# Sparse attention and a mixture of experts: stage two asks for each split weight one product ahead, and the planner's costs of a weight's scale change

## The chip, the cores and the metric

The kernel runs on one core of one Trainium2 chip. The metric is the device time of one execution in microseconds (us). TensorE (PE) multiplies matrices and loads their weights, VectorE (DVE), ScalarE (ACT) and GpSimd (POOL) work on tiles, and SyncE (SP) issues the DMAs.

## What is computed

First attention over blocks, for 4 batches of 8 heads, 768 positions and 64 values a head; then its result x, 3072 rows of 512, goes through a gate that is balanced over rows and columns, and through all 8 experts. Cut to what matters:

```python
scores = np.where(mask, scale * np.matmul(q, k.T), -1e9)     # mask from sampled_blocks
attn = softmax(scores) @ v                                   # -> x, 3072 x 512
logits = x @ w_gate
P = np.exp(logits - logits.max())
for _ in range(8):
    P /= P.sum(1, keepdims=True) + 1e-09
    P /= P.sum(0, keepdims=True) + 1e-09
    P *= N / E
for e in range(E):
    h = np.maximum(x @ w1[e], 0.0)                           # w1[e]: 512 x 1024
    out += P[:, e:e + 1] * (h @ w2[e])                       # w2[e]: 1024 x 512
```

## The kernel before

**Numbers.** Every float32 operand is split into two float16 parts, a high and a low one, and a product is three matmuls (high x high, high x low, low x high). A 2 x 2 block product is made from seven products of sums of blocks instead of eight; they are numbered 0 to 6 and run in the order 0, 1, 5, 6, 3, 4, 2. So each expert has seven split weights `w1p` and seven `w2p`, and each batch of x has seven split inputs `xp`.

**The attention** is written out by hand as a table of turns: `at(T, rank, function)`. At turn -20 the scale of the first q and k (`scale_qk`, L619 to L626) is made on DVE, and at turn -21 `lay_fence` (L488 to L515) builds the mask's fence from the sampled blocks, also on DVE. The q and k of the first head are then cast (ACT, L640), split (DVE, L644) and turned by DMA (L650).

**The experts.** A step i is expert e = i // 4 and batch b = i % 4. `stage1(i, qi)` makes a quarter of h: seven products into PSUM tiles `p` (L1192; four banks), which DVE and ACT combine (L1204, L1239), and ten or so operations on POOL and DVE that form and split seven `h` tiles. `stage2(i, p)` multiplies the `h` of product p with `w2p[p]` for three pairs of row tiles (L1309, PSUM tiles `py`, four banks) and DVE adds each into `acc` (L1332; in the first expert ACT writes the first product's, L1329). The main loop (L1372) runs the seven stage2 products of step i, with the four quarters of stage1 of step i + 1 between them, so PE has both kinds of work at hand.

**The change of expert.** In the last batch of an expert the next w2 is loaded (L177) and measured: eight partial maxima on ACT (L108, `mx_w`), the maximum of the eight on DVE (`whole`, L194, `ma_w`), its spread over all partitions by a transposition on PE into a `p` bank (`spread`, L114, `all_w`), and seven small DVE operations that make the scale (`power`, L200 to L206, `sw`). POOL forms the five sums of blocks that the seven products need (L1071, into `r` and `t`), and for each product ACT writes the high half of `w2p[p]` (L1056) and DVE the low half (L1060). w1 goes the same way (`arena` and `attic` are its split tiles).

**The planner.** These steps stand in a queue (`Slots`). `tick` is called once after each product, with the time that PE and DVE are taken to need; a step of the lazy queue is run at a tick when its turn has come, when `gap` ticks have passed since the last lazy step, and when the engine that it costs is not more than 1.0 us ahead of PE by the planner's account (`fits`). A step planned with no cost always fits. `need(key)` runs all that stands in the queue up to that key at once. `stage2(i, p)` needs the split of product p right before its matmuls. `not_earlier` keeps a step of a weight behind what its engine has in the program ahead of it, and a scheduler then orders each engine's instructions.

## Time and profile before

| | us |
|---|---|
| median of 3 runs | 2264.57 |
| lowest and highest | 2260.46, 2267.06 |
| the profiled execution | 2263.39 |
| its span | 2261.6 |
| PE busy | 2168.9 (96%) |
| DVE busy | 1883.2 (83%) |
| ACT, POOL busy | 1317.3 (58%), 1309.7 (58%) |
| stage two's matmuls, L1309, x8064 | 946.3 |
| stage one's matmuls, L1192, in four groups of one shape, the three largest | 411.5, 409.7, 146.3 |

A busy time is the union of an engine's instructions, so PE lacks 93 us of the span. A share of the whole span says little here: attention, the first expert and the later experts have different limits, and a wait counts only where PE has nothing else to run.

### The profile page before, as it was taken

What the parts mean: (1) busy time and instruction counts of PE and PEld (TensorE: products, weight loads), DVE (VectorE), ACT (ScalarE), POOL (GpSimd) and SP (SyncE); (2) the same over time, 40 slices, a digit from 0 to 9 for tenths busy, and PEclk for the clock granted to TensorE, in tenths of its full rate; (3) what the DMA queues carried; (4) which work ended last, traced back from release to release, by engine and by line L of the source; (5) the groups of instructions that cost most, each with busy time, mean ns of one, the idle gap of its engine ahead of it and who ended that gap; (6) DMA issues with size and microseconds to landing.
All of it is one profiled execution on the core that took longest, in us unless ns stands there. A gap on an engine that the chain in (4) does not pass through costs nothing.

```text
span 2261.6 us, 47616 instructions
## 1 busy us (share of the span) xinstructions
PE 2168.9 (96%) x18892; PEld 1599.6 (71%) x18892; DVE 1883.2 (83%) x3339; ACT 1317.3 (58%) x2435; POOL 1309.7 (58%) x1331
## 2 busy tenths in 40 slices
PE   6999999889998999999999999999999999999999
PEld 3777666657775777677777777777777777777777
DVE  8889999787888878887888788878887888788876
ACT  5998888755457644654465446544654465446442
POOL 2123445585548564866486648655866586658553
PEclk9999999999999999999999999999999999999999
DMA  7667866313112211221212121212121212121221
GB/s 165 138 141 152 199 131 141 122 57 115 50 50 87 87 50 66 71 87 50 84 53 87 50 87 50 87 50 87 50 87 50 87 50 87 50 87 57 78 78 50
DMA packets 195349, 192.39 MB, mean 85 GB/s; under 512 B 132124, under 2 KB 150580, under 8 KB 195124
## 3 DMA queue, kind: packets, MB, share of 16 engines
q1 hardware_dynamic: 194560, 189.30, 28.9%
q8 instruction: 148, 2.42, 0.4%
q14 instruction: 77, 0.63, 0.1%
q10 hardware_dynamic: 564, 0.03, 0.0%
HBM read 140.54 MB, written 17.30 MB: 70 GB/s over the span
## 4 chain that ended last, share of the span: by engine, by line
PE 72%; DVE 11%; POOL 9%; ACT 4%; issue 3%; DMA 1%; SPq 0%; POOLq 0%; DVEq 0%
PE py L1309 31%; PE p L1192 31%; POOL r L1071 3%; PE u L753 3%; DVE top L671 2%; POOL h L1224 2%; PE t L695 2%; PE t L698 2%; PE m L662 2%; PE m L665 2%; DVE acc L1332 1%; DVE attic L1060 1%; POOL s L1266 1%; DVE h L1224 1%; POOL a L1078 1%
## 5 line engine op out<-in xcount | busy, mean ns | idle before, releaser
L1309 PE MATMUL py<-w2p,h 128*128 128x256 f16 x8064 | 946.3, 273 | 30.3 <-DVE acc L1332 14.1
L1309 PEld LDWEIGHTS <-h 128*128 128x128 f16 x8064 | 788.2, 98 | 166.5 <-issue 32.1
L1332 DVE SCALAR_TENSOR_TENSOR acc<-py,spare,acc 128x256 f32<-128x256 f32 (+1 forms) x840 | 455.6, 580 | 61.4 <-PE py L1309 57.8
L1224 POOL TENSOR_TENSOR h<-u,h 128x384 f16<-128x384 f32 x128 | 118.7, 928 | 583.5 <-ACT h L1214 566.7
L1192 PEld LDWEIGHTS <-attic 128*128 128x128 f16 x3072 | 300.4, 98 | 191.7 <-issue 12.8
L1192 PE MATMUL p<-arena 128*128 128x384 f16 x2304 | 411.5, 327 | 9.0 <-DVE arena L1060 4.4
L1192 PE MATMUL p<-attic 128*128 128x384 f16 x2304 | 409.7, 326 | 5.4 <-ACT a L1239 2.0
L1192 PEld LDWEIGHTS <-arena 128*128 128x128 f16 x2304 | 225.6, 98 | 144.0 <-issue 9.6
L1214 ACT ACTIVATE h<-c 128x384 f16<-128x384 f32 x256 | 133.2, 520 | 313.8 <-DVE c L1204 240.4
L1204 DVE SCALAR_TENSOR_TENSOR a<-p,a 128x384 f32<-128x384 f32 x384 | 210.8, 549 | 20.3 <-PE p L1192 15.3
L671 DVE TENSOR_REDUCE top<-m 128x1 f32<-128x768 f32 x192 | 181.7, 951 | 27.8 <-PE m L665 26.8
L703 ACT ACTIVATE pe<-t,qk 128x768 int32<-128x768 f32 x192 | 172.3, 898 | 47.0 <-PE t L698 44.5
L1214 ACT ACTIVATE h<-r 128x384 f16<-128x384 f32 x256 | 132.2, 519 | 64.2 <-POOL r L1078 59.7
L1078 POOL TENSOR_TENSOR c<-c,r 128x384 f32<-128x384 f32 x128 | 158.9, 1242 | 10.0
L1078 POOL TENSOR_TENSOR r<-s,r 128x384 f32<-128x384 f32 x128 | 153.2, 1197 | 10.0
L1192 PE MATMUL p<-arena,attic 128*128 128x384 f16 x768 | 146.3, 326 | 3.8 <-DVE a L1204 3.8
L1204 DVE SCALAR_TENSOR_TENSOR r<-p,a 128x384 f32<-128x384 f32 x128 | 70.7, 552 | 93.5 <-PE p L1192 73.7
L1214 ACT ACTIVATE h<-s 128x384 f16<-128x384 f32 x128 | 66.8, 522 | 134.4 <-POOL s L1266 134.4
L1266 POOL TENSOR_TENSOR s<-a,u 128x384 f32<-128x384 f32 x128 | 134.5, 1051 | 17.5 <-ACT a L1263 17.4
L1078 POOL TENSOR_TENSOR a<-a,r 128x384 f32<-128x384 f32 x128 | 135.8, 1061 | 9.4
L662 PE MATMUL m<-kt,qt 128*128 128x512 f16 (+1 forms) x384 | 128.4, 334 | 11.0 <-DMA kt<-ks 7.9
L1071 POOL TENSOR_TENSOR r<-r 128x256 f32<-128x256 f32 (+1 forms) x106 | 119.5, 1145 | 33.0 <-DVE arena L1060 33.0
(206 smaller groups left out, 3736.9 us busy)
## 6 DMA issues: line engine op xcount, KB each, us to landing
arena<-xd SPq DMA_DIRECT2D x128, 384.0 KB, 4.0
attic<-xd SPq DMA_DIRECT2D x96, 384.0 KB, 4.1
r<-in_moe_w_dram SPq DMA_DIRECT2D x16, 2048.0 KB, 9.1
arena<-in_q_dram SPq DMA_DIRECT2D x16, 384.0 KB, 4.4
arena<-in_k_dram SPq DMA_DIRECT2D x16, 384.0 KB, 4.6
arena<-in_v_dram SPq DMA_DIRECT2D x4, 1536.0 KB, 8.3
xd<-xs_t SPq DMA_DIRECT2D x16, 384.0 KB, 3.5
out_dram<-acc SPq DMA_DIRECT2D x48, 128.0 KB, 1.7
```

Of the source, the lines that this page charges most:

```text
L662: nc.tensor.matmul(sc[:, lo:hi], lhsT=qt[:, 0, c], rhs=ka[:, lo:hi], start=True, stop=False)
L671: nc.vector.tensor_reduce(out=tops[n][:, c : c + 1], in_=sc[:, :S], axis=AX.X, op=ALU.max)
L703: nc.scalar.activation(pe, sc[:, :S], AF.Exp, bias=EXP_SHIFT, scale=qk[n // 2][3])
L1071: lambda c=c: Pinned.gpsimd.tensor_tensor(out=out[:, c], in0=x[:, c], in1=y[:, c], op=op),
L1078: nc.gpsimd.tensor_tensor(out=out, in0=x, in1=y, op=ALU.subtract)
L1192: nc.tensor.matmul(ps, lhsT=w1p[p][:, l, kc, fs], rhs=xp[p][:, r, kc], start=(kc == 0 and m == 0), stop=(kc == KH - 1 and m == 2),)
L1204: nc.vector.scalar_tensor_tensor(out=t, in0=ps, scalar=HDOWN, in1=other, op0=ALU.mult, op1=ALU.add)
L1214: nc.scalar.activation(h[:, 0], src, AF.Relu if relu else AF.Copy)
L1224: eng.tensor_tensor(out=h[:, 1], in0=src, in1=h[:, 0], op=ALU.subtract)
L1266: nc.gpsimd.tensor_tensor(out=s1, in0=a1, in1=u3, op=ALU.add)
L1309: nc.tensor.matmul(py, lhsT=hs[i, p, kc][:, l, tsl], rhs=w2p[p][:, r, kc], start=(kc == 0 and m == 0), stop=(kc == KF // 2 - 1 and m == 2),)
L1332: nc.vector.scalar_tensor_tensor(out=dst, in0=src, scalar=c, in1=dst, op0=ALU.mult, op1=ALU.add)
```

## The change

Four lines. `lay_fence` moves from turn -21 to -20. The maximum of the eight partial maxima is queued without a cost (0.1 us of DVE before), and the spread of every weight follows after a gap of 5 ticks, that of the second expert's w2 too (14 before). And in an expert's first batch (`b == 0`) `stage2` needs the split of its own product and that of the one after it in the order 0, 1, 5, 6, 3, 4, 2.

```diff
-        at(-21, LATER, lay_fence)
+        at(-20, LATER, lay_fence)
@@ scale_w
-        slots.add(whole, key, 1, True, dve=0.1)
-        slots.add(spread, key, 1, True, gap=14 if which == 2 and e == 1 else 5)
+        slots.add(whole, key, 1, True)
+        slots.add(spread, key, 1, True, gap=5)
@@ stage2
+    SECOND = (0, 1, 5, 6, 3, 4, 2)
+
     def stage2(i, p):
         e, b = divmod(i, B)
         if p not in (0, 1, 3):
             slots.need(("sum", i))
         slots.need(("h", i, p))
-        slots.need(("w2", e, p))
+        ahead = SECOND.index(p)
+        for k in SECOND[ahead : ahead + 2 if b == 0 else ahead + 1]:
+            slots.need(("w2", e, k))
```

Since four lines are added, a line of the kernel before from L1294 on stands four lines later in the changed one (L1309 is L1313, L1332 is L1336).

**DVE at the change to the fifth expert** (e = 4, i = 16). w2p_8081 is the split weight of product 0 and w2p_8082 that of product 1; r_17_0, a_17_0 and u_17_0 are combinations of the quarter of stage one that runs beside it, h_... low halves of h, and acc_8118<-py_0_... the accumulations of product 0. Before:

```order
L1060 SCALAR_TENSOR_TENSOR w2p_8081<-r_4_18880,sw_4_18885,w2p_8081 128x1024
L1224 TENSOR_TENSOR h_8105<-s_16_3_19436,h_8105 128x384
L1204 SCALAR_TENSOR_TENSOR u_17_0_19597<-p_17_0_19598,a_17_0_19568 128x384
...
L1332 SCALAR_TENSOR_TENSOR acc_8118<-py_0_0_19471,spare_19467,acc_8118 128x512 x2
L1332 SCALAR_TENSOR_TENSOR acc_8118<-py_0_1_19487,spare_19467,acc_8118 128x512 x2
L1332 SCALAR_TENSOR_TENSOR acc_8118<-py_0_2_19503,spare_19467,acc_8118 128x512 x2
L1060 SCALAR_TENSOR_TENSOR w2p_8082<-r_4_18880,sw_4_18885,w2p_8082 128x1024
```

Now, on the same engine at the same place:

```order
L1060 SCALAR_TENSOR_TENSOR w2p_8081<-r_4_18880,sw_4_18885,w2p_8081 128x1024
L1060 SCALAR_TENSOR_TENSOR w2p_8082<-r_4_18880,sw_4_18885,w2p_8082 128x1024
L1204 SCALAR_TENSOR_TENSOR r_17_0_19586<-p_17_0_19587,a_17_0_19577 128x384
L1204 SCALAR_TENSOR_TENSOR a_17_0_19577<-p_17_0_19597,a_17_0_19577 128x384
L1336 SCALAR_TENSOR_TENSOR acc_8118<-py_0_0_19477,spare_19467,acc_8118 128x512 x2
```

The split of product 1 has moved from behind all six accumulations of product 0 to a place ahead of them and ahead of the combinations r_17_0 and a_17_0.

**PE at the change to the second expert** (e = 1, i = 4). all_w_1 is the spread of the maximum of w2, p_4_2, p_4_3 and p_5_0 are products of three successive quarters of stage one. Before:

```order
L1192 MATMUL p_4_3_11328<-attic 128x384
L1192 LDWEIGHTS attic
L1192 MATMUL p_4_3_11328<-attic 128x384
L114 MATMUL all_w_1_11353<-ident,ma_w_1_10790 128x128
L1192 LDWEIGHTS arena
```

Now:

```order
L1192 MATMUL p_4_2_11158<-attic 128x384
L1192 LDWEIGHTS attic
L1192 MATMUL p_4_2_11158<-attic 128x384
L114 MATMUL all_w_1_11224<-ident,ma_w_1_10790 128x128
L1192 LDWEIGHTS arena
```

The spread has moved from the end of quarter p_4_3 to its beginning, 42 matmuls earlier. At the experts after the third the same instruction of w2 moves 106 matmuls earlier, to a place in front of the third quarter; there the 36 matmuls of product 4 and two of product 2 of stage two, which came beside and behind that quarter, now stand ahead of it.

**DVE at the start.** L619 is the first operation of the scale of the first q and k, L490 the first of the fence. Now:

```order
L481 TENSOR_SCALAR qs_109<-attic 128x24 x6
L619 TENSOR_REDUCE qk_0_178<-u_143 128x2
L620 TENSOR_SCALAR qk_0_178<-qk_0_178 128x2
L622 TENSOR_SCALAR qk_0_178<-qk_0_178 128x2
L623 RECIPROCAL qk_0_179<-qk_0_178 128x2
L624 TENSOR_SCALAR qk_0_179<-qk_0_179 128x2
L625 TENSOR_SCALAR qk_0_178<-qk_0_178 128x2
L626 TENSOR_SCALAR qk_0_180<-qk_0_178 128x1
L490 CAST attic<-attic 24x72
```

Before, L490 followed L481, and the scale came after all of the fence.

## Rows read from the trace of the kernel before

**Rows 1.** Stretches in us: length, busy per engine (instructions), clock, DMA share, GB/s.
```profile
440.00:530.00 90.00, 78.96 (x557) 54.97 (x554) 72.25 (x116) 52.89 (x104) 68.62 (x66) 0.98 0.24 86
...
690.00:720.00 30.00, 21.76 (x130) 13.35 (x129) 24.21 (x42) 24.38 (x55) 28.82 (x30) 0.89 0.30 93
...
880.00:980.00 100.00, 92.99 (x702) 68.39 (x701) 87.85 (x150) 60.31 (x120) 70.27 (x67) 1.00 0.15 53
...
1335.00:1435.00 100.00, 95.30 (x720) 69.89 (x718) 90.21 (x154) 57.12 (x114) 72.17 (x69) 1.00 0.15 50
```

The engines stand in the order PE, PE's weight loads, DVE, ACT, POOL.

**Rows 2.** Timeline of PE, fifth expert: start, us, instruction, count, [idle before, releaser].
```profile
1364.33 3.09 PE L1192 MATMUL p<-arena 128*128 128x384 f16 x18
...
1403.25 3.76 PE L1309 MATMUL py<-w2p,h 128*128 128x256 f16 x33 [1.18 <-DVE w2p L1060]
...
1417.19 1.47 PE L1309 MATMUL py<-w2p,h 128*128 128x256 f16 x12 [1.69 <-DVE acc L1332]
...
1424.51 0.92 PE L1309 MATMUL py<-w2p,h 128*128 128x256 f16 x7 [0.97 <-ACT w2p L1056]
...
2079.29 3.76 PE L1309 MATMUL py<-w2p,h 128*128 128x256 f16 x33 [1.19 <-DVE w2p L1060]
```

**Rows 3.** Timeline of DVE, fifth expert.
```profile
1397.43 4.03 DVE L1332 SCALAR_TENSOR_TENSOR acc<-py,spare,acc 128x512 f32<-128x512 f32 x6
1401.38 1.82 DVE L1060 SCALAR_TENSOR_TENSOR w2p<-r,sw,w2p 128x1024 f16<-128x1024 f32 x1
```

**Rows 4.** Timeline of ACT, fifth expert.
```profile
1367.21 0.63 ACT L108 ACTIVATE unread<-r 128x512 bf16<-128x512 f32 x1
1367.75 0.19 ACT L108 ACTIVATION_READ_ACCUMULATOR unread<-r 128x1 f32 x1
...
1388.13 1.15 ACT L1056 ACTIVATE w2p<-r,sw 128x1024 f16<-128x1024 f32 x1
```

**Rows 5.** Line L1060: count, duration in ns min/median/max, first and last start.
```profile
L1060 DVE SCALAR_TENSOR_TENSOR w2p<-r,sw,w2p x48: 1266/1451/2093, 468.2 to 2111.7; 128x1024 f16<-128x1024 f32 x48
```

**Rows 6.** The stretch around the fifth expert's splits, columns as in rows 1.
```profile
1388.20:1424.50 36.30, 32.48 (x246) 23.86 (x244) 33.75 (x52) 19.09 (x34) 35.67 (x35) 1.00 0.04 16
```

**Rows 7.** Tile mx_w (the partial maxima): its reader, columns as in rows 5.
```profile
L194 DVE TENSOR_REDUCE ma_w<-mx_w x16: 142/152/163, 301.3 to 2056.2; 128x1 f32<-128x8 f32 x16
```

**Rows 8.** Waits of PE from 880 to 980: us in total, times, longest.
```profile
PE py L1309 <- DVE acc L1332: 3.0, 2, 1.7
PE py L1309 <- DVE w2p L1060: 1.7, 1, 1.7
```

**Rows 9.** Timeline of PE, second expert.
```profile
690.60 3.09 PE L1192 MATMUL p<-attic 128*128 128x384 f16 x18
...
709.08 0.47 PE L114 MATMUL all_w<-ident,ma_w 128*128 128x128 f32 x1 [7.16 <-DVE ma_w L194]
```

**Rows 10.** Timeline of ACT, second expert.
```profile
696.25 0.52 ACT L1214 ACTIVATE h<-c 128x384 f16<-128x384 f32 x1
696.68 0.61 ACT L108 ACTIVATE unread<-r 128x512 bf16<-128x512 f32 x1
```

**Rows 11.** Timeline of POOL, second expert.
```profile
702.54 1.00 POOL L1078 TENSOR_TENSOR c<-c,r 128x384 f32<-128x384 f32 x1
```

**Rows 12.** One microsecond after that wait, columns as in rows 1.
```profile
709.00:710.00 1.00, 0.92 (x4) 0.53 (x5) 0.75 (x2) 1.00 (x3) 0.92 (x2) 0.50 0.00 0
```

**Rows 13.** Timeline of PE, first expert.
```profile
486.06 1.47 PE L1309 MATMUL py<-w2p,h 128*128 128x256 f16 x12 [0.54 <-ACT w2p L1056]
...
498.32 1.15 PE L1192 MATMUL p<-arena,attic 128*128 128x384 f16 x5 [2.67 <-DVE a L1204]
```

**Rows 14.** Timeline of DVE, first expert.
```profile
491.82 0.56 DVE L1204 SCALAR_TENSOR_TENSOR c<-p,u 128x384 f32<-128x384 f32 x1 [2.66 <-POOL s L1266]
...
494.60 2.02 DVE L1060 SCALAR_TENSOR_TENSOR w2p<-t,sw,w2p 128x1024 f16<-128x1024 f32 x1
```

**Rows 15.** Timeline of DVE, start.
```profile
11.90 0.62 DVE L644 SCALAR_TENSOR_TENSOR qs<-arena,qk,qs 128x384 f16<-128x384 f32 x1 [0.68 <-ACT qs L640]
```

## The prediction

> **What bounds the kernel now.** I read the stretches of the span first, to see where TensorE (PE) is not busy, and then the timeline of PE with the releaser of each wait. From 40 us on PE is nearly always busy, and what it lacks lies where one expert's weights give way to the next: 11.0 of 90 us at the first expert, 8.2 of 30 us at the second, 7.0 of 100 us at the third and 4.7 of 100 us at the fifth [rows 1]. The fifth stands for five: the wait at 1403.25 comes again at 2079.29, three experts later [rows 2], a period of 225.3 us. Its waits in stage two are three: 1.18 us for VectorE's (DVE) half of the split weight of product 1, 1.69 us for an accumulation on DVE, and 0.97 us for ScalarE's (ACT) half of the split of product 3 [rows 2], together 3.84 us. Between these changes PE runs full. So the change can move only these places, and the start of the kernel, where the fence stands.
>
> **The fourth to the eighth expert (e = 3 to 7, five times): the split asked for one product ahead.** The piece of the order on DVE shows the effect: before, the low half of w2p_8082 (product 1) stands behind six accumulations of product 0, which take 4.03 us, and then takes 1.82 us itself [rows 3]; PE waits 1.18 us for it. Now it stands directly behind w2p_8081, ahead of those six. That wait goes, and so does the 0.97 us one of product 3, whose ACT half now is made a product earlier. What comes: ACT makes the two high halves back to back, and one takes 1.15 us [rows 4]. PE now asks for the second one after only three matmuls of product 0 (the order of PE has the first matmul of product 1 there). ACT begins the pair in the last product group of the quarter before, as it did with the first one, so between 0 and 1.15 us of the second is exposed; I take 0.7 us, nearer the full piece since nothing stands between the two. What stays: the six accumulations of 4.03 us now come behind one more split, whose median is 1.45 us [rows 5], and so do the combinations of stage one that free PE's four banks for p. In the stretch around this DVE is busy 33.75 of 36.30 us [rows 6], so it has 2.55 us to give. The 1.69 us wait for DVE therefore stays, under this name or as a wait for a bank of p. The sum is -1.18 - 0.97 + 0.70 = -1.45, taken as -1.5 us for each expert. Bounds: -3.8 us, if all three waits go and DVE carries its backlog past the end of the stretch; and +1.3 us, if both early splits take the 2.09 us maximum in place of the 1.45 us median. Five times: -7.5 us (-19 to +6.5).
>
> The planner's dropped 0.1 us for the maximum also moves work here. The reduction L194 is run as soon as the eight partial maxima are out, and five ticks later the transposition L114 on PE: in the order it stands 106 matmuls earlier. Its price on PE is the same. Whether PE now waits at it is told by rows: it stands behind the 18 products that began at 1364.33 before, with 38 matmuls of stage two (3.76 / 33 = 0.11 us each) drawn ahead of them, so PE comes to it at 1364.33 + 4.1 = 1368.4 [rows 2]; the eighth partial begins at 1367.21 and takes 0.63 and a read of 0.19 [rows 4], and L194 0.15 [rows 7], so 1368.2. It fits, by 0.2 us. I cost it at nothing; the cover is those 38 matmuls. The queue of SyncE changes too: the load of the next w1 is issued ahead of two or four loads of x. PE waits for no DMA in these stretches, and these loads belong to a batch that PE begins only after two more products of stage two; nothing.
>
> **The third expert.** It has the same three waits with larger numbers, and two more: DVE accumulations and splits are waited for 3.0 and 1.7 us [rows 8], of 7.0 in all [rows 1]. I take -1.5 as above and half of the rest beyond the three (2.6 us, whose order changes because its w1 maximum comes some 230 matmuls earlier): -2.8 us (-7 to +1).
>
> **The second expert: the gap of 14 ticks becomes 5.** Here is a loss. Before, PE comes to the transposition after the quarter p_4_3 and waits 7.16 us, until 709.08 [rows 9]. Now the transposition stands one quarter (42 products) earlier, in front of p_4_3, as the order shows. PE reaches that place at 690.60 + 3.09 = 693.7 [rows 9]. But the partials begin on ACT only at 696.68 [rows 10], and in the new order ACT runs the eight between casts that wait for the four results of GpSimd (POOL) in this quarter; the last of these ends at 702.54 + 1.00 = 703.54 [rows 11]. Then come a cast (0.52), the eighth partial (0.61 + 0.19) and L194 (0.15): 705.0. PE waits from 693.7 to 705.0. The 42 products, 42 x 3.09 / 18 = 7.2 us, follow it, so the next quarter starts at 712.2 plus the transposition, where it started at 709.08 plus the transposition: +3.1 us. Bounds: 0, if ACT gets its partials done early enough, and +7.2, a whole quarter. The granted clock is 0.50 (1.2 GHz of 2.4) after the wait of before [rows 12]; the longer wait will meet it as well, so I count no difference.
>
> **The first expert.** The 0.54 us wait for ACT's split goes [rows 13]. But PE now has two matmuls of p_1_2 ahead of 33 of product 5, and their bank is freed by DVE's combination of 491.82, itself held 2.66 us by POOL [rows 14]. PE comes there at about 486.06 - 0.54 + 0.98 (the group p2 moved ahead) + 15 x 0.11 = 488.2 and waits until 491.82 + 0.56 = 492.4, some 4.2 us. In return the 2.67 us wait at 498.32 [rows 13] goes, since the combination it needs no longer stands behind the 2.02 us split of 494.60 [rows 14]. 4.2 - 2.67 - 0.54 = +1.0 us (-3 to +3).
>
> **The start.** The scale of the first q and k goes ahead of the fence on DVE. Before, the split that follows both began at 11.90, after 0.68 us of waiting for ACT's cast [rows 15]. DVE now does the fence's work while ACT casts, so the splits gain at most that wait: -0.3 us (-0.7 to 0).
>
> **Sum.** -7.5 - 2.8 + 3.1 + 1.0 - 0.3 = -6.5 us. The profiled execution took 2263.39 us (1.8 more than its span), 1.2 below the median of the three runs shown, so 2263.4 - 6.5 = 2256.9: 2257 us.
>
> **Rivals.** *DVE is the bound, and nothing is saved.* For it: 33.75 of 36.30 us busy [rows 6]; the order puts two splits in a row in front of everything else on DVE while POOL makes its sums of w2, and a split costs 1.27 to 2.09 us [rows 5]. If each of two early splits takes the maximum instead of the median, that is 2 x 0.64 = 1.3 us an expert, about what I credit; then the third to the eighth expert give 0, and 2263.4 + 3.1 + 1.0 - 0.3 = 2267 us is left. The Trainium skill (GPSIMD Engine Reference, Key points) says that GpSimd shares its SBUF interfaces with VectorE and contends with VectorE instructions that have two SBUF inputs; the split is such an instruction, and the spread of its times agrees. By that rule this rival would be the result, at the same 2267 us. Against it: at 1401.38 the split already took 1.82 us [rows 3], so part of the price is paid before.
>
> *All three waits go.* For it: the new order of PE no longer breaks products of stage two into pieces of one matmul as often, so fewer waits fall into a short cover. At most 3.8 us for each of five and 5 us at the third: 2263.4 - 19 - 5 + 3.1 + 1.0 - 0.3 = 2243 us.
>
> *The transposition stops PE at every expert.* The margin of 0.2 us above is one ACT instruction wide, and ACT's partials stand among casts that wait for POOL. If the eighth partial ends later than I count, PE, whose queue holds all products behind L114, waits in full. From 2.5 us an expert (six of them) the result is slower: 15 us against the -6.5, with the gains kept, is 2272 us; at 4 us, 2281. For it: the second expert shows such a wait of 7.16 us [rows 9]. Against it: 38 matmuls were put in front of it here.
>
> *The change does not do what it says.* The queue only keeps a split from running earlier than its place, so it could still run late. The order of DVE and ACT shows that it does not; I give it no chance of its own.
>
> **How the numbers follow.** Forecast 2257 (2252 to 2262): 0.45. DVE is the bound, 2267 (2262 to 2271): 0.25. All waits go, 2243, or most of them (2243 to 2252): 0.20. The transposition stops PE, 2272 and more: 0.10. The range leaves out half of the last and a part of the third: 2246 to 2268. A measurement of this kernel tells about 0.3% from no change, 6.8 us: faster is below 2257.8, slower above 2271.4. The forecast lies on that line, so a little over half of its chance (0.26) counts as faster: 0.46 faster, 0.44 the same, 0.10 slower.
>
> **What would show it.** At the second expert, one PE wait at L114 of about 11 us instead of 7.16: if it is at or under 7, my loss there is wrong. At the fourth to the eighth expert, no wait for w2p over 0.7 us and a period shorter than 225.3 by 1 to 2 us: if it is unchanged, DVE is the bound; if PE waits at L114, it is the third rival. At the first expert, a wait of some 4 us near 488 us in place of the one at 498. The prediction fails most easily in the period of these five, which counts five times.

## The result and the profile after

The changed kernel takes 2274.05 us (median of six runs, 2271.62 to 2278.15), the kernel before in the same session 2264.22: a ratio of 1.0043, 95% interval 1.0032 to 1.0054. It is 9.8 us slower, where 6.5 us less was forecast.

The profiled execution has a span of 2274.4 us, 12.8 more than before. The stretches of the changed kernel at the second and the fifth expert, which answer to two of [rows 1], with one more behind the second (columns as there: length, then busy us of PE, PE's weight loads, DVE, ACT, POOL; clock, DMA share, GB/s):

```profile
690.00:720.00 30.00, 17.99 (x96) 10.08 (x95) 16.13 (x34) 20.61 (x46) 18.01 (x17) 0.77 0.30 93
720.00:760.00 40.00, 35.67 (x273) 26.31 (x271) 36.68 (x57) 21.70 (x39) 35.54 (x35) 1.00 0.00 1
1345.00:1445.00 100.00, 95.97 (x712) 68.96 (x711) 90.57 (x149) 56.59 (x111) 70.03 (x66) 1.00 0.15 50
```

The second expert's stretch stands out: PE lacks 12.0 of 30 us where it lacked 8.2, and DVE is busy 16.1 us where it was 24.2. The fifth expert's lack fell from 4.7 to 4.0 us, and yet its period grew. PE's ends are modelled, so some 0.16 us of each stop show as a longer matmul and not as idle time, and many small stops count more than the idle column says. Hence this table goes from mark to mark: the first matmul of stage one, then the end of the seventh split of w1 of each next expert on DVE, then PE's last matmul, all in us from the timelines. A column from the second on holds one change of expert.

| kernel | 1st | 2nd | 3rd | 4th | 5th | 6th | 7th | 8th |
|---|---|---|---|---|---|---|---|---|
| before | 250.7 | 222.4 | 223.6 | 225.3 | 225.4 | 225.3 | 225.4 | 233.5 |
| changed | 250.9 | 231.3 | 224.8 | 226.2 | 226.3 | 226.2 | 226.2 | 233.5 |
| e1 ahead | 250.9 | 222.3 | 223.7 | 225.5 | 229.1 | 225.5 | 225.5 | 233.6 |
| e2 free maximum | 250.5 | 226.8 | 226.0 | 227.4 | 228.1 | 228.1 | 228.1 | 236.2 |
| e3 changed, gap 14 | 251.2 | 226.1 | 225.0 | 225.4 | 225.4 | 225.5 | 226.2 | 234.3 |
| e4 fence | 252.7 | 224.1 | 223.6 | 225.4 | 225.4 | 225.5 | 225.4 | 233.5 |
| e5 free maximum, gap 12 | 251.0 | 226.8 | 223.0 | 225.7 | 225.8 | 225.8 | 225.7 | 233.9 |
| e6 free maximum, bank read early | 252.5 | 226.8 | 225.2 | 225.7 | 226.4 | 226.8 | 226.5 | 235.3 |
| e9 ahead, gap 12 | 252.3 | 221.6 | 221.6 | 223.6 | 223.6 | 222.8 | 222.9 | 231.8 |
| e11 free maximum, bank of py | 249.1 | 226.6 | 224.4 | 228.5 | 228.5 | 228.3 | 228.5 | 236.6 |
| e13 changed, gap 12 | 251.1 | 226.6 | 221.1 | 222.9 | 222.9 | 223.7 | 223.6 | 231.7 |

The changed kernel lost 8.9 us at the second expert, 1.2 at the third, 0.8 to 1.0 at each of the next four, 0.1 at the eighth, and 0.2 at the first: 13.9, less 1.0 in attention. The time up to the first matmul of stage one differs from one execution to the next by up to 10 us (422.8 to 432.6 us over these kernels), so a kernel is compared by its median, and its parts by this table. In the first two columns a difference of under 2 us tells nothing: e4, whose edit lies in front of all experts, differs there by 2.0 and 1.7 us from the kernel before. The period is what the fourth to the seventh column hold.

The second expert, PE's timeline, and a window of all engines behind the wait (717.99 is the first product of stage two behind the transposition):

```profile
689.77 3.09 PE L1192 MATMUL p<-attic 128*128 128x384 f16 x18
704.30 0.48 PE L114 MATMUL all_w<-ident,ma_w 128*128 128x128 f32 x1 [11.45 <-DVE ma_w L194]
...
717.99 0.49 PE L1313 MATMUL py<-w2p,h 128*128 128x256 f16 x3
...
733.53 1.14 PE L1192 MATMUL p<-arena,attic 128*128 128x384 f16 x6 [0.78 <-DVE a L1204]
735.62 2.14 PE L1192 MATMUL p<-attic 128*128 128x384 f16 x12 [0.95 <-ACT a L1239]
...
748.31 2.78 PE L1313 MATMUL py<-w2p,h 128*128 128x256 f16 x24 [1.26 <-DVE acc L1336]
...
752.00 2.79 PE L1313 MATMUL py<-w2p,h 128*128 128x256 f16 x24 [0.91 <-DVE acc L1336]
```

```profile
704.00:710.00 6.00, 5.70 (x19) 2.88 (x20) 0.72 (x2) 1.19 (x4) 0.63 (x1) 0.52 0.32 74
```

PE waits 11.45 us at the transposition, against 7.16 in [rows 9]. Then the others are empty: in the six microseconds after it DVE works 0.72 us, ACT 1.19, POOL 0.63, because all they could do hangs on products that PE didn't make. PE itself has the half clock there (0.52), as in [rows 12]. Six later waits of 0.43 to 1.26 us (four are shown) follow: from 712 on, what DVE, ACT and POOL could not do in the pause is missing.

The fifth expert, PE's timeline:

```profile
1371.83 6.93 PE L1313 MATMUL py<-w2p,h 128*128 128x256 f16 x62
1378.60 0.27 PE L114 MATMUL all_w<-ident,ma_w 128*128 128x128 f32 x1
...
1388.08 1.47 PE L1313 MATMUL py<-w2p,h 128*128 128x256 f16 x12
1389.39 3.09 PE L1192 MATMUL p<-arena 128*128 128x384 f16 x18
...
1395.88 1.14 PE L1192 MATMUL p<-attic 128*128 128x384 f16 x6 [0.43 <-DVE a L1204]
...
1401.52 0.49 PE L1313 MATMUL py<-w2p,h 128*128 128x256 f16 x3
1402.56 5.37 PE L1313 MATMUL py<-w2p,h 128*128 128x256 f16 x45 [0.55 <-ACT w2p L1056]
...
1416.86 1.14 PE L1192 MATMUL p<-arena 128*128 128x384 f16 x6 [0.82 <-DVE a L1204]
1418.47 3.76 PE L1313 MATMUL py<-w2p,h 128*128 128x256 f16 x33 [0.47 <-DVE w2p L1060]
...
1433.03 0.27 PE L1313 MATMUL py<-w2p,h 128*128 128x256 f16 x1 [0.53 <-ACT w2p L1056]
```

The three waits of [rows 2] are gone. Five small ones stand there, two of them for combinations (DVE a) that free a bank of p, and those were no waits before. And between the third quarter of stage one and the fourth (the row at 1388.08) only 12 matmuls of stage two are left. In the kernel before, the same place reads:

```profile
1371.92 7.26 PE L1309 MATMUL py<-w2p,h 128*128 128x256 f16 x65
```

What the lost cover costs at its place can be read from start to start: the 66 matmuls of stage one between these 12 and the next ones of stage two take PE 12.13 us (1389.39 to 1401.52). In the kernel before the same 66 take 10.83 us, with a transposition of 0.11 us among them. That is 1.4 us more.

### The profile page after: what moved, and what is told of

It is laid out like the page before. It is cut to its first block, busy times and chain, and to the rows that moved or that the text cites. A ratio compares the mean times of both kernels' runs of the same rounds, so it can differ in the third digit from the quotient of the medians.

```text
span 2274.4 us, 47580 instructions
## 1 busy us (share of the span) xinstructions
PE 2176.4 (96%) x18892; PEld 1598.1 (70%) x18892; DVE 1888.9 (83%) x3339; ACT 1323.4 (58%) x2435; POOL 1309.1 (58%) x1331
## 4 chain that ended last, share of the span: by engine, by line
PE 66%; DVE 15%; POOL 10%; ACT 4%; issue 3%; DMA 1%; SPq 0%; POOLq 0%; DVEq 0%; ACTq 0%
PE py L1313 30%; PE p L1192 27%; POOL r L1071 3%; PE u L753 2%; DVE acc L1336 2%; DVE top L671 2%; POOL h L1224 2%; DVE h L1224 2%; PE t L695 2%; PE t L698 2%; PE m L662 1%; PE m L665 1%; DVE attic L1060 1%; POOL t L1071 1%; POOL s L1266 1%
## 5 line engine op out<-in xcount | busy, mean ns | idle before, releaser
L1313 PE MATMUL py<-w2p,h 128*128 128x256 f16 x8064 | 944.1, 273 | 23.6 <-ACT w2p L1056 9.3
L1313 PEld LDWEIGHTS <-h 128*128 128x128 f16 x8064 | 787.6, 98 | 160.9 <-issue 25.4
L1336 DVE SCALAR_TENSOR_TENSOR acc<-py,spare,acc 128x256 f32<-128x256 f32 (+1 forms) x840 | 456.9, 580 | 44.1 <-PE py L1313 39.7
L1224 POOL TENSOR_TENSOR h<-u,h 128x384 f16<-128x384 f32 x128 | 136.0, 1063 | 594.8 <-ACT h L1214 577.7
L1192 PEld LDWEIGHTS <-arena 128*128 128x128 f16 x2304 | 225.5, 98 | 157.6 <-issue 21.9
L1078 POOL TENSOR_TENSOR c<-c,r 128x384 f32<-128x384 f32 x128 | 149.8, 1171 | 10.0
L1266 POOL TENSOR_TENSOR s<-a,u 128x384 f32<-128x384 f32 x128 | 129.3, 1010 | 17.0 <-ACT a L1263 17.0
L1224 POOL TENSOR_TENSOR h<-r,h 128x384 f16<-128x384 f32 x128 | 133.2, 1040 | 6.6 <-ACT h L1214 6.6
```

The costliest lines, as they stand in the source:

```text
L1078: nc.gpsimd.tensor_tensor(out=out, in0=x, in1=y, op=ALU.subtract)
L1192: nc.tensor.matmul(ps, lhsT=w1p[p][:, l, kc, fs], rhs=xp[p][:, r, kc], start=(kc == 0 and m == 0), stop=(kc == KH - 1 and m == 2),)
L1224: eng.tensor_tensor(out=h[:, 1], in0=src, in1=h[:, 0], op=ALU.subtract)
L1266: nc.gpsimd.tensor_tensor(out=s1, in0=a1, in1=u3, op=ALU.add)
L1313: nc.tensor.matmul(py, lhsT=hs[i, p, kc][:, l, tsl], rhs=w2p[p][:, r, kc], start=(kc == 0 and m == 0), stop=(kc == KF // 2 - 1 and m == 2),)
L1336: nc.vector.scalar_tensor_tensor(out=dst, in0=src, scalar=c, in1=dst, op0=ALU.mult, op1=ALU.add)
```

## The experiments

Times are medians beside the kernel before in the same session; ratios with their 95% intervals.

**e1_ahead** has only the edit of `stage2` (need the split of the next product too).

> The kernel before with the split asked for one product ahead, and nothing else of the change. Its order leaves every spread of a maximum where it was before. My theory: asking ahead is what lengthens the later experts, since two splits in a row on ACT and DVE hold back the combinations that free the banks of p. Then the period of the fourth to the eighth expert is 226.2 us as in the changed kernel (225.3 before), and waits of PE for DVE's a and ACT's w2p stand there again. The second expert is as before: one wait of 7.2 us at L114, no loss of 8.9 us. The sum is 2264 + 6 x 0.9 = 2269 us. The rival, that the earlier spread (it holds one of four banks of p) lengthens the period: then this kernel keeps 225.3 us or less, some 224 us by my prediction, and gives 2257 to 2264 us.

Measured: 2265.29 against 2264.79 us, 1.0003 (0.9989 to 1.0017). The second expert is as before; the period is 225.5 us. Its waits at the fourth expert:

```profile
1181.79 5.03 PE L1313 MATMUL py<-w2p,h 128*128 128x256 f16 x42 [1.02 <-DVE acc L1336]
...
1190.74 2.78 PE L1313 MATMUL py<-w2p,h 128*128 128x256 f16 x24 [1.80 <-DVE acc L1336]
...
1197.52 2.67 PE L1313 MATMUL py<-w2p,h 128*128 128x256 f16 x23 [0.51 <-DVE w2p L1060]
```

That is 3.33 us in place of 3.84, with more hidden stops: asking ahead alone moves the waits and gains nothing. Nor is it what lengthens the period, so my theory fell. (The 229.1 us at the fifth expert go with one split on DVE, that of product 0 at 1404.74, which took 6.07 us in place of 2.11.)

**e2_free_max** has only the maximum without its cost.

```diff
-        slots.add(whole, key, 1, True, dve=0.1)
+        slots.add(whole, key, 1, True)
```

> The kernel before with the maximum queued at no cost, and nothing else; the gap of 14 for the second expert stays. In its order the spread of w2 stands 106 matmuls earlier at the fourth to the eighth expert, as in the changed kernel, and at the second expert 6 matmuls earlier. My theory (asking ahead lengthens the period): the period stays at 225.3 us within 0.2, PE does not wait at L114 there, the second expert's wait at L114 stays at 7 us within 1, sum 2262 to 2266 us. The rival (the earlier spread lengthens the period): 226.2 us a period, sum 2268 to 2271 us.

Measured: 2284.42 against 2264.79 us, 1.0088 (1.0071 to 1.0104). The edit that I had costed at nothing is the slowest of all: 228.1 us a period, where even the rival had 226.2. PE's timeline at the fifth expert, a window behind its last wait, and the timeline at the sixth:

```profile
1382.42 1.47 PE L1309 MATMUL py<-w2p,h 128*128 128x256 f16 x12
...
1408.62 5.54 PE L1309 MATMUL py<-w2p,h 128*128 128x256 f16 x34 [2.22 <-DVE w2p L1060]
```

```profile
1410.00:1413.00 3.00, 3.00 (x16) 2.17 (x15) 3.00 (x3) 0.14 (x1) 3.00 (x3) 0.52 0.00 0
```

```profile
1636.70 3.87 PE L1309 MATMUL py<-w2p,h 128*128 128x256 f16 x34 [2.22 <-DVE w2p L1060]
...
1659.38 1.03 PE L1309 MATMUL py<-w2p,h 128*128 128x256 f16 x8 [0.80 <-ACT w2p L1056]
```

PE doesn't wait for the spread here. The same 12 matmuls are left between the quarters, and the 66 behind them take 12.14 us, as in the changed kernel: 1.4 of the 2.7 us. Behind the wait of 2.22 us the clock was halved at the fifth expert: 16 matmuls at 0.21 us from start to start, where 0.11 is usual, 1.6 us in all. That is no part of the price. At the sixth and the seventh expert the same wait stands and PE runs on at the full clock (34 matmuls in 3.87 us, not 5.54), and the period is 228.1 us all the same: three waits (0.80 us for ACT, 0.36 and 0.19 for combinations) stand a little later, where the fifth expert has none.

**e3_gap14** is the changed kernel with the gap of 14 back.

```diff
-        slots.add(spread, key, 1, True, gap=5)
+        slots.add(spread, key, 1, True, gap=14 if which == 2 and e == 1 else 5)
```

> The changed kernel with the gap of 14 ticks for the second expert's w2 put back; all else of the change stays. Theory: the 8.9 us that the second expert lost come from the place of this one spread, a quarter early. Then PE's wait at L114 is 7 us within 1 in place of 11.45, the waits of 0.4 to 1.3 us behind it are gone, and the time is 2274 - 8.9 = 2265 us (2263 to 2268). The rival, that asking ahead makes the loss in the second expert: the time stays at 2271 us or more, and waits for w2p and acc remain behind the transposition.

Measured: 2269.81 us, 1.0024 (1.0014 to 1.0035). Of the 8.9 us at the second expert 5.2 are back, not all:

```profile
715.23 0.47 PE L114 MATMUL all_w<-ident,ma_w 128*128 128x128 f32 x1 [8.03 <-DVE ma_w L194]
...
737.88 1.80 PE L1313 MATMUL py<-w2p,h 128*128 128x256 f16 x15 [1.14 <-ACT w2p L1056]
...
747.62 1.47 PE L1313 MATMUL py<-w2p,h 128*128 128x256 f16 x12 [1.42 <-DVE acc L1336]
```

The other 3.7 go with what e3 keeps, most likely the free maximum, which even with the gap of 14 puts the spread six matmuls earlier (e2 has 4.4 there). The gap is nothing without it: the kernel before with a gap of 5 has the very order that it has with 14.

**e4_fence** has only the fence's turn.

> The kernel before with the fence laid one turn later, and nothing else. Theory: the gain of 2 us that the changed kernel has by 60 us comes from this alone, so the first products of scores start some 0.5 us earlier and PE's mark at 60 us is 1.5 to 2.5 us earlier; the experts run as before (period 225.3 us). Time 2261 to 2264 us. The rival, that the 2 us are a difference between two executions (the granted clock between 20 and 40 us was 0.83 and 0.91): the mark is anywhere, and the time is that of before.

Measured: 2264.88 us, 1.0000 (0.9991 to 1.0009). The first product of scores starts at 17.90 us, as in the changed kernel (17.89), against 18.38 before: 0.5 us from the fence. The theory of the 2 us at 60 us fell: e4 is 0.2 us ahead there, and six kernels without this edit (e1 and e2 among them) are 1.5 us ahead. Most of the 2 us is a difference between executions.

**e5_gap12** is e2 with a gap of 12 for the later w2.

```diff
-        slots.add(spread, key, 1, True, gap=14 if which == 2 and e == 1 else 5)
+        slots.add(spread, key, 1, True, gap=14 if which == 2 and e == 1 else (12 if which == 2 else 5))
```

> The kernel with only the maximum at no cost, and the spread of each w2 after a gap of 12 ticks in place of 5 (14 at the second expert as before). The spread stays early (99 matmuls earlier than in the kernel before, at the fourth to the eighth expert), but 65 matmuls of stage two stand again between the quarters p_16_2 and p_16_3; with the gap of 5 only 12 stood there. My theory now: what the early maximum costs is this cover, since the spread takes its bank in turn with the products of p, and whatever of stage two was ready is drawn in front of it; DVE, ACT and POOL then have the next quarter before they are done with the last. Then the period is 225.3 us again, within 0.5, in place of 228.1. The rival, that the early spread itself costs (it holds one of the four banks of p until the scale is made): the period stays at 227.5 us or more.

Measured: 2271.37 against 2263.32 us, 1.0037 (1.0023 to 1.0051). By the table 4.4 us are lost at the second expert; the period is 225.75. Timelines of PE and POOL, fifth expert:

```profile
1352.60 0.82 PE L1192 MATMUL p<-arena 128*128 128x384 f16 x4 [0.50 <-DVE arena L1060]
...
1381.05 6.50 PE L1309 MATMUL py<-w2p,h 128*128 128x256 f16 x58
...
1409.80 2.45 PE L1309 MATMUL py<-w2p,h 128*128 128x256 f16 x21 [2.12 <-DVE w2p L1060]
```

```profile
1390.63 3.10 POOL L1071 TENSOR_TENSOR t<-r 128x256 f32<-128x256 f32 x4
```

The spread is as early as in e2 (113 and 106 matmuls ahead of its old place; the 99 of the expectation was miscounted), 58 matmuls of stage two stand between the quarters again, the 66 behind them take 10.72 us (1387.38 to 1398.10), and 2.3 of the 2.7 us are gone. The spread holds its bank as long as in e2 all the while: from the transposition to DVE's read of it (L200) pass 11.5 us here and 11.3 in e2. So the bank held is not what makes e2 long. The half clock costs nothing here either: at the seventh expert it follows the wait of 2.1 us, at the fifth and sixth it doesn't, and the three periods are 225.7 to 225.8 us.

**e6_early_read** frees the spread's bank early.

```diff
         def spread():
-            wr["all", which] = spread_max(a, f"w{which}_{e}")
+            whole_w = spread_max(a, f"w{which}_{e}")
+            vector.tensor_reduce(out=a, in_=whole_w, axis=AX.X, op=ALU.max)
```

> The kernel with only the maximum at no cost (gap of 5), and the spread's bank is read by DVE right behind the transposition, so that the bank is held for about 1 us in place of 11.4. Its order still has the stage-two products in front of the spread. If the bank held is what costs, the period falls from 228.1 to 225.3 us. If it is the cover between the quarters, it stays at 227.3 to 228.3 us. I expect the second.

Measured: 2277.05 us, 1.0061 (1.0040 to 1.0081); the period is 225.7 to 226.8 us, between the two. But the order moved too: 26 matmuls stand between the quarters, not 12. So this run doesn't part the bank from the cover.

**e7_act_ahead** asks ahead for ACT's half alone (its steps get a key of their own, which `stage2` needs one product ahead).

> The kernel before with only ACT's half of the split asked for one product ahead; DVE's half stays at its own product. If the place of DVE's half is what gives back the gain of asking ahead (three waits of 3.3 us stand in the place of 3.8), then here the wait of 0.97 us for ACT goes and the two for DVE stay at 1.2 and 1.7: period 224.3 us, time 2258 to 2261 us. If DVE is simply behind in this stretch by as much as PE waits, the period stays at 225.2 to 225.6 us and the waits for DVE grow by what ACT's loses.

Measured: 2265.90 us, 1.0010 (1.0001 to 1.0020), period 225.6 (226.2 at the seventh expert). The wait for ACT fell to 0.42 us, those for DVE grew from 2.87 to 3.38 (the longest to 2.10), and the sum stayed: 3.80 us. DVE is behind by what PE waits.

**e8_no_low_1** is e1 without one DVE instruction a change.

```diff
+        if key[0] == "w2" and key[1] and key[2] == 1:
+            return
         slots.add(
             lambda: Pinned.vector.scalar_tensor_tensor(
```

> Left out: the low half of product 1's split weight of w2 on DVE, in the second to the eighth expert, that is one DVE instruction of 1.3 to 2.1 us at each change of expert; the output is therefore not the reference's there. All else is the kernel with the split asked for one product ahead. If DVE's work in this stretch is the bound, PE's waits at each change fall by about that instruction: period 225.6 - 1.5 = 224.1 us (223.6 to 224.5). If it is the order of the waits and not the amount of DVE's work, the period stays within 0.3 of 225.6 us.

Measured: 2260.48 us, 0.9990 (0.9980 to 1.0000). The sixth and the seventh expert take 223.9 us, as the bound by DVE says, the fourth and fifth 226.4 and 225.2. In these two PE waits 3.1 us for the split of product 0, because this one instruction takes DVE 5.1 us in place of 2.1 (timelines of PE and DVE, fifth expert, then sixth):

```profile
1406.81 0.92 PE L1315 MATMUL py<-w2p,h 128*128 128x256 f16 x7 [3.12 <-DVE w2p L1062]
```

```profile
1401.65 5.10 DVE L1062 SCALAR_TENSOR_TENSOR w2p<-r,sw,w2p 128x1024 f16<-128x1024 f32 x1 [2.57 <-ACT w2p L1056]
```

```profile
1638.48 2.78 PE L1315 MATMUL py<-w2p,h 128*128 128x256 f16 x24 [1.54 <-DVE acc L1338]
```

```profile
1626.89 2.11 DVE L1062 SCALAR_TENSOR_TENSOR w2p<-r,sw,w2p 128x1024 f16<-128x1024 f32 x1 [2.57 <-ACT w2p L1056]
```

Where that split takes its usual time, the period is 1.6 us under e1's 225.5: the instruction left out is saved time, so DVE's work is the bound in that order. The eighth expert has a long split too (5.11 us). What held these splits up stays open.

**e9_ahead_gap12** joins e1 with e5 and leaves w1 and the second expert alone.

```diff
-        slots.add(whole, key, 1, True, dve=0.1)
-        slots.add(spread, key, 1, True, gap=14 if which == 2 and e == 1 else 5)
+        slots.add(whole, key, 1, True, dve=0.0 if which == 2 and e > 1 else 0.1)
+        slots.add(spread, key, 1, True, gap=14 if which == 2 and e == 1 else (12 if which == 2 else 5))
```

> The split asked for one product ahead, the maximum of w2 at no cost from the third expert on with a gap of 12 ticks (cover between the quarters kept), w1 and the second expert as before. If the cover is what the free maximum costs and asking ahead takes the wait for w2p that the gap of 12 alone kept (2.1 us at 1409.8), the period is 225.4 us or less, the second expert loses nothing, and the time is 2264 us, within 3. If something else of the early maximum costs, the period is 226 us or more and the time is 2269 us or more.

Measured: 2250.31 against 2263.42 us, 0.9940 (0.9926 to 0.9955): faster than both kernels. I had expected no gain; the period is 222.8 to 223.6 us. PE's timeline and POOL's, fifth expert:

```profile
1370.62 6.50 PE L1313 MATMUL py<-w2p,h 128*128 128x256 f16 x58
...
1388.51 5.25 PE L1313 MATMUL py<-w2p,h 128*128 128x256 f16 x45 [0.35 <-ACT w2p L1056]
...
1402.25 3.76 PE L1313 MATMUL py<-w2p,h 128*128 128x256 f16 x33 [0.67 <-DVE w2p L1060]
...
1412.55 1.14 PE L1192 MATMUL p<-attic 128*128 128x384 f16 x6 [0.89 <-DVE a L1204]
```

```profile
1380.24 3.10 POOL L1071 TENSOR_TENSOR t<-r 128x256 f32<-128x256 f32 x4
1383.30 2.10 POOL L1071 TENSOR_TENSOR r<-r 128x256 f32<-128x256 f32 x3
```

The waits are 1.91 us in place of 3.84. POOL makes its first sums 38.1 us after the period's first wait; in the kernel before they begin 48.9 us after it, behind an idle time of POOL:

```profile
1386.92 0.91 POOL L1224 TENSOR_TENSOR h<-u,h 128x384 f16<-128x384 f32 x1 [5.21 <-ACT h L1214]
...
1393.20 3.42 POOL L1071 TENSOR_TENSOR t<-r 128x256 f32<-128x256 f32 x4
```

So an early spread lets these sums fill the idle 5.21 us, and the splits have their sources earlier. (In e5 they begin as early, 38.0 us after the first wait, without a gain.) Asking ahead is worth 2.1 to 2.9 us a period here (against e5) and nothing where the spread is late (e1).

**e10_py_bank** takes the spread's bank from py in the kernel before.

```diff
-    spread_bank[0] = lambda nm: ps_h.tile([P, 512], F32, tag="ph", name=nm)
+    spread_bank[0] = lambda nm: ps_y.tile([P, 512], F32, tag="py", name=nm)
```

> The kernel before, with one edit: the spread takes one of the four banks of py in place of one of p. The theory on the order says that what shares the spread's banks is drawn behind it and the rest in front. In this order the spread of the second expert's w2 stands 18 products of stage one later than before, and stage two of the last batch stands between the quarters p_4_1 and p_4_3 in place of ahead of them; from the third expert on the order is that of the kernel before. By the theory the wait of 7.16 us at L114 shrinks by at least the 18 products, 2.9 us, and no period changes: 2264 - 3 to 2264 - 7, that is 2257 to 2261 us. The rival, that the place of the spread in the second expert is no matter as long as it isn't early, because its chain of maximum, scale and split ends when it ends: the wait moves to the first split w2p and the time is that of before, 2264 us within 2.

Measured: 2265.60 us, 1.0004 (0.9993 to 1.0015). PE's timeline, first spread of w1, then that of w2:

```profile
659.13 0.45 PE L114 MATMUL all_w<-ident,ma_w 128*128 128x128 f32 x1 [10.62 <-DVE ma_w L194]
...
711.59 0.27 PE L114 MATMUL all_w<-ident,ma_w 128*128 128x128 f32 x1
```

My 2257 to 2261 us fell. The spread of w2 stands 18 matmuls (three products; the expectation calls them 18 products) later. Its 7.16 us are gone, and 10.62 stand at that of w1, which this edit put about a hundred matmuls earlier. The same trap at another place.

**e11_free_max_py** is e2 with the bank of e10.

> The maximum at no cost, with the spread in a bank of py. The order now has three quarters of stage one (p_16_1 to p_16_3) with no product of stage two between them, at each change from the third expert on, and the spread early. If the missing cover is what lengthens the period, it is longer than the 228.1 us of the early spread in a bank of p: 229 to 233 us, with waits of PE for DVE's and ACT's combinations in the second and third of these quarters. If the bank of p held by the spread is the cause, the period is back at 225.3 us.

Measured: 2281.40 us, 1.0080 (1.0062 to 1.0097), period 228.3 to 228.5 us. No bank of p is held, and the period is as long as in e2: a held bank of p is not the cause. The waits stand in the quarters without cover, as expected (here 0.50, 0.24, 0.52 and 0.92 us; two are shown), though the total came out half a microsecond under the range.

```profile
1364.60 1.14 PE L1192 MATMUL p<-attic 128*128 128x384 f16 x6 [0.50 <-DVE a L1204]
...
1371.63 3.09 PE L1192 MATMUL p<-attic 128*128 128x384 f16 x18 [0.92 <-ACT a L1239]
```

This run also parts the cover from POOL's sums of w2, which an early spread brings forward. Counted from the wait for `arena` that opens the period, they begin after 37.3 us here, 38.0 in e5, 42.5 in e2 and 48.9 in the kernel before. So e11 and e5 have them at nearly the same place, and their periods are 2.7 us apart; what differs is the cover, none against 58 matmuls, and the spread's bank, which is one of py here. PE's and POOL's timelines of e11:

```profile
1348.73 0.82 PE L1192 MATMUL p<-arena 128*128 128x384 f16 x4 [0.50 <-DVE arena L1060]
```

```profile
1386.07 2.78 POOL L1071 TENSOR_TENSOR t<-r 128x256 f32<-128x256 f32 x4
```

**e12_ahead_py** is e10 with e1.

> The split asked for one product ahead, and the spread in a bank of py. By the theory the two are independent: the time is that of the kernel with the spread in a bank of py and nothing else, within 2 us, since asking ahead by itself changes the period by 0.1 to 0.2 us. If asking ahead gains once the second expert's wait is gone, it is 2 us or more below.

Measured: 2265.48 us, 1.0017 (1.0004 to 1.0030), period 225.5: asking ahead adds nothing here either.

**e13_changed_gap12** alters one number of the changed kernel.

```diff
-        slots.add(spread, key, 1, True, gap=5)
+        slots.add(spread, key, 1, True, gap=12 if which == 2 else 5)
```

> The changed kernel with one number altered: the spread of every w2 follows the maximum after 12 ticks in place of 5. All else of the change stays: the fence, the maximum at no cost for both weights, the split asked for one product ahead. If the lost cover between the quarters is why the changed kernel is slow from the third expert on, the period falls from 226.2 to 223.0 us (222.6 to 223.7) here too, and the second expert, where the spread now stands 18 products before its old place, still loses some 3 to 6 us. Sum: 2274 - 5 x 3 - 3 = 2256 us (2253 to 2260). If it needs the old handling of w1 or of the second expert, the period stays at 225.4 us or more and the time at 2267 us or more.

Measured: 2254.19 against 2263.43 us, 0.9964 (0.9945 to 0.9983). The changed kernel was 9.8 us over the kernel before; with this number it is 9.2 under it. The period is 222.9 to 223.7 us, and the second expert, whose spread stands 18 matmuls early (again not 18 products), still loses 4.2. PE's timeline, fifth expert:

```profile
1370.13 6.50 PE L1313 MATMUL py<-w2p,h 128*128 128x256 f16 x58
1376.47 3.09 PE L1192 MATMUL p<-arena 128*128 128x384 f16 x18
...
1387.19 0.49 PE L1313 MATMUL py<-w2p,h 128*128 128x256 f16 x3
```

The 66 matmuls behind the cover take 10.72 us again, where the changed kernel needs 12.13: 1.4 of the 2.5 to 3.5 us by which a period is shorter. The time lies in the range that the theory of the cover gave (2253 to 2260 us).

**e14_best_py1** is e9 with the bank of py for the second expert's w2 alone.

> The split asked for one product ahead, the gap of 12 from the third expert on, and the spread of the second expert's w2 alone in a bank of py, so that it stands 24 matmuls of stage one later. If a spread that stands too early costs what PE idles at it, the wait at L114 falls from 7.16 us by 3.9 to about 3.2 and the time from 2250.3 to 2246 us (2244 to 2249). If the chain of maximum, scale and split sets the end of this stretch, the wait moves to the first w2p of the second expert and the time stays at 2250 us within 1.5.

Measured: 2248.92 us, 0.9931 (0.9913 to 0.9949), not to be told from e9.

```profile
707.21 0.48 PE L114 MATMUL all_w<-ident,ma_w 128*128 128x128 f32 x1 [2.28 <-DVE ma_w L194]
```

The wait is 2.28 in place of 7.16 us, and the second expert takes 222.3 us against 221.6. In both kernels the transposition comes 33.45 us after the wait for `arena` that opens this stretch. So the chain of load, partial maxima, scale and split sets the end here, as the second case said, and PE's waits move behind it (1.46 and 0.74 us for acc).

## Why the prediction was wrong, point by point

**The planner's free maximum: the step that failed.** The text said "I cost it at nothing; the cover is those 38 matmuls". It asked one question, whether PE would wait at the earlier transposition, and got that right: in the trace PE reaches it without a wait from the third expert on. (The text puts the transposition behind the 18 products that began at 1364.33; the order has it in front of them, and the sum, 1368.4, counts it there.) It did not ask what those matmuls of stage two had covered at their old place. They stood between two quarters of stage one, where DVE, ACT and POOL finish the one before the next. Stage two drawn ahead leaves 12 there of 65. e2 puts the price of this edit alone at 2.1 to 2.8 us a change, 4.4 at the second expert. By the matmuls between the quarters, without asking ahead: 65 give 225.3 us (late spread), 58 give 225.75, 26 give 226.5, 12 give 228.1, none gives 228.4. That the cover is the cause, and not the bank held, is shown by e5 and e11; e11 beside e5 shows that it isn't the place of POOL's sums either. With the gap of 12 in the changed kernel, which brings the cover back (e13), the periods are 222.9 to 223.7 us, where the forecast of -1.5 us meant 223.8.

**The split asked for ahead: a term mis-sized.** -1.5 us for each of five was forecast; alone it is +0.1 to +0.2 (e1), within the bounds. On top of the free maximum it is -1.2 to -2.7 (from e2 to the changed kernel and to e3). Taken in the other order, the free maximum on top of asking ahead is 0 to +0.7 (from e1 to the same two). So neither single price is that part's share of the loss. The rival that DVE is the bound, at 2267 us, describes e1 (2265.29) well. What I credited, the waits of 1.18 and 0.97 us, did go, and waits for accumulations took their place. The rule of the Trainium skill that was put beside that rival (GPSIMD Engine Reference, Key points: GpSimd and VectorE contend at SBUF where a VectorE instruction has two inputs there) is neither borne out nor refuted by these runs: no run changed POOL's work alone. The median of the splits (line L1060, as in [rows 5]) is 1.285 us in e9 against 1.451 before, but 1.411 in e5, where POOL's sums begin as early as in e9.

**What the parts do together.** I added the parts up, and they don't add: with the gap of 5, ahead and free maximum give 0.1 to 1.0 us a period, where one alone gives 0.2 and the other 2.7; with the gap of 12 they give -1.6 to -2.5, where the free maximum alone gives +0.4. Beside an early spread asking ahead is worth 1.2 to 2.9 us, whether the cover is there (e5 to e9) or not (e2 to the changed kernel and e3), and the cover is worth 1.7 to 2.4 us without asking ahead (e2 to e5) and 1.8 to 3.5 with it (e3 and the changed kernel to e13). So the gain that I had credited to asking ahead exists where the spread is early, and brings the kernel under the one before only with the cover.

**The second expert.** The wait was forecast at 11.3 us, ending at 705.0; it is 11.45, ending at 704.3. But its price was put at +3.1 us (up to 7.2), the shift of one quarter, and it is +8.9. The shift itself came out right: from the mark that opens this change (677.59 us before, 676.75 now) the first product of stage two behind the transposition starts 3.3 us later (717.99; the row of the kernel before stands below). The step that failed is that the sum ends with "the 42 products follow it": it counted PE's time alone. While PE stands, DVE and POOL run dry, and the other 5.6 us come as waits when PE is back. Only 5.2 of the 8.9 belong to the gap (e3).

```profile
715.55 4.20 PE L1309 MATMUL py<-w2p,h 128*128 128x256 f16 x37
```

**The third expert**: -2.8 forecast, +1.2 measured; most likely the same cause as in the later ones, since e13 has 2.5 us less than the kernel before there. **The first expert**: +1.0 forecast, +0.2 measured, not to be told from none by a column in which e4 differs by 2.0. The wait of 4 us near 488 did not come: PE ran the 33 matmuls of product 5 from 488.01 on without one, so the bank it needed was free, and the wait of 2.67 us became four of 0.5 to 1.2. **The start**: -0.3 forecast, -0.5 measured. **The transposition stops PE at every expert**, the rival on the slower side, names the right edit with the wrong mechanism: PE waits at no transposition of w2 from the third expert on, and that its 2272 us lie near the 2274 measured is luck.

## What to carry to other kernels

When a change draws work forward, ask what it covered at its old place, not only whether it is in time at the new one: here a step that no engine waits for cost 2.7 us a turn because other work went ahead of it (e2). A pause of the busiest engine costs more than its length if the others live on its results. And parts of a change that meet in one queue are not to be added up from their single prices; run the one number that sets the place (here the gap) at two or three values before the rest is judged. A slow stretch of one engine isn't a cost by itself: e2 and e5 have periods with the half clock and without, of one length, because PE would have waited for DVE and ACT soon after.

## What the runs showed of the hardware

The same order of instructions ran at two speeds: from the third expert on the changed kernel and e3 have one order, and a period is 226.2 us in the one and 225.45 in the other, three times, then 226.2. The difference is a wait of 0.53 us for ACT's split that is there or not. In e2 the half clock followed a wait of 2.22 us, with 0.60 shortly before it, at the fourth, the fifth and the eighth expert, and the same two waits at the sixth and the seventh did not bring it; a wait of 1.69 us in the kernel before did not either. Where it came, in e2's fifth and e5's seventh expert, the period was no longer than where it didn't. One DVE split of product 0 took 6.07 us in e1 and three took 5.10 to 5.11 in e8, in place of 2.11. In e1 the trace shows one instruction transfer of 0.02 MB in that stretch, in e8's fifth expert none, so what delayed them is not settled.
